# The last eight columns of T from on-chip tiles, and spread single-column products, in a Fourier-filter and feed-forward kernel

## The chip, the cores and the metric

The kernel runs on one core of a Trainium2 chip. The metric is the device time of one execution in microseconds. Before the change three runs took 1841.04, 1837.14 and 1839.90 us; their median is 1839.90.

## What is computed

The input x has 8192 tokens of 448 channels. A row c of 448 numbers makes six modulation rows. First comes a layer norm, scaled and shifted by two of them, then a Fourier filter over the tokens with a small complex network per frequency, and then a layer norm and a gated feed-forward network:

```python
mod = (_silu(c) @ w_mod).reshape(c.shape[0], 6, 1, -1)
sa, ca, ga, sb, cb, gb = (mod[:, 0], mod[:, 1], mod[:, 2], mod[:, 3], mod[:, 4], mod[:, 5])
h = _layernorm(x, axis=-1) * (1 + ca) + sa
x = x + ga * _A_ref(h, A_w1, A_b1, A_w2, A_b2)   # rfft2, two complex layers in 4 blocks of 112, soft threshold, irfft2
h = _layernorm(x, axis=-1) * (1 + cb) + sb
x = x + gb * _B_ref(h, B_w_gate, B_w_up, B_w_down)   # (gelu(h @ w_gate) * (h @ w_up)) @ w_down
```

## The kernel before, in words

The transform of 8192 = 128 x 64 tokens is made in two steps. The **first stage** takes x as 64 *columns* of 128 tokens each. Column b lies in chunk b // 4; a chunk is a tile xt of 128 partitions, four columns and 448 channels, and there are 16. For each column VectorE (or ScalarE for a few) makes the statistics of the layer norm; for a group of columns a chain on ScalarE (q, a square root) and VectorE gives the factor y (L421 to L427); an engine scales the 128-point matrix by y (fr, L190); TensorE multiplies the column by it (dft_a, L199, product at L201); and ScalarE copies the product back over the column, with a correction mu for the mean (out_a, L204; means, L208, product at L210). The result, called T, so stands in the tiles xt: 128 rows of frequencies by 64 columns.

T is also stored to DRAM (td), because the second stage needs it with the columns on the partitions. store_t (L366) writes a chunk: the first four chunks whole, of the others at first only quarter c = 0, the tile's partitions 0, 4, 8 and so on, which are T's rows 0 to 31 in td. The other quarters are written later, in the second stage.

The order of all of the first stage is made by a small planner. task (L377) notes an engine, a cost, a due time and what a step depends on; in_order (L387) plays the tasks through and gives one order, which is written out as it stands. Beside the columns the planner places:

- mod_terms on VectorE (L225) and mod_cols (L261, product at L266): eight products of one column each, which turn the modulation rows sa and ca into columns. bounds1, scale_sum (L299), scale_of and modulated make the scale of the first network layer and its scaled weights w1m; weights1_hi and weights1_lo split these into two float16 parts.
- dc_cols (L276, product at L281): eight more products of one column, for the term of frequency zero.
- the stores of all 16 chunks, issued on SyncE.

Behind the planner's tasks, in the order in which the code is written, stand the steps that open the **second stage** (L795 on). It works on 32 *units* (h, bt), a half of the channels and a block of eight rows of T. fetch_t (L504) loads a unit's tile tr from td: partitions 0 to 63 are the 64 columns for one row parity o, 64 to 127 those for the other, and along a partition lie four rows of 224 channels. There are three tr buffers; they come from a pool that is opened after the first stage's pool `ap` is closed and takes its place in memory. The first three units are fetched at L796. Then mod_row (L237, product at L247) makes the modulation rows sb and cb, four products each; row_copy and weights2_hi prepare the second network layer, and split_t (L519) splits units 0 and 1 into float16 parts th and tl on ScalarE and VectorE. From then on step (L733) takes one unit after another: it fetches unit i + 2, makes the 64-point transform of unit i (stage_s2), splits unit i + 1 on GpSimd, and runs the network and the inverse transform for the units before (stage_m1, stage_m2, stage_i1). On TensorE the order at the start is: transform of unit 0, of unit 1, first layer of unit 0, transform of unit 2, second layer of unit 0 (L626 to L633). weights2_lo and weights2_turn give that layer's low part w2l; its turn on GpSimd (L333, L334) stands behind the split of unit 2.

SyncE issues every transfer in one queue. There are eight semaphores for them, so a transfer waits until the one eight places ahead of it has landed.

Later stages, which the change doesn't touch, load and pack the feed-forward weights, finish the inverse transform and run the feed-forward network.

Of the kernel before, what the change touches and what calls it, by code (L numbers as in the profile page):

```python
# [12 lines left out]
F16 = mybir.dt.float16  # L13
# [37 lines left out]
def spectral_geglu(ctx, tc, x, wa, wb, wg, wu, wd, cvec, wmod, wmod3, cf1, cs2, cmi, cgm, out):  # L51
    nc = tc.nc
    V, S, G, T = nc.vector, nc.scalar, nc.gpsimd, nc.tensor
    dma = nc.sync.dma_start
# [5 lines left out]
    td = dram.tile([128, NB, D], F32, name="td")  # L60
# [9 lines left out]
    def bank(tag, name):  # L70
        return (psumc if tag == "pc" else psum).tile([128, 512], F32, tag=tag, name=name)
# [72 lines left out]
    with ExitStack() as actx:  # L144
        ap = actx.enter_context(tc.tile_pool(name="ap", bufs=1, side="right"))
        xts = {}
# [41 lines left out]
        frs, psb, psu = {}, {}, {}  # L188
# [48 lines left out]
        def mod_row(h, ks):  # L237

            if h not in rps:
                rps[h] = bank("pd", "psm")  # L240
            for k in ks:
                c = slice(2 * h, 2 * h + 2)
                if k < 3:
                    a, w = cs[:, k : k + 1].to_broadcast([128, 128]), wn[:, c, k]
                else:
                    a, w = cs[64:128, 3:4].to_broadcast([64, 128]), w3[64:128, c]
                T.matmul(rps[h][:, :D].rearrange("p (h c) -> p h c", h=2), a, w, start=k == 0, stop=k == 3)  # L247
# [5 lines left out]
        sa0 = lp.tile([112, NBLK], F32, name="sa0")  # L253
# [4 lines left out]
        wsc = cpool.tile([128, 2], F32, name="wsc")  # L258
        col2 = mpool.tile([113, 1], F32, name="col2")

        def mod_cols():  # L261

            ps = bank("pc", "psm")
            psu["m"] = ps
            for b in range(2 * NBLK):
                T.matmul(  # L266
                    ps[:112, b : b + 1], ms[:, b // 2, b % 2 * BS : (b % 2 + 1) * BS], ones[:, 0:1], start=True, stop=True
                )
# [4 lines left out]
            V.tensor_scalar(sa0, ps[:112, 0:4], float(N) * 2.0**-ZSC, None, op0=ALU.mult)  # L273
            V.tensor_scalar(ca1[:112], ps[:112, 4:8], 1.0, None, op0=ALU.add)

        def dc_cols():  # L276

            ps = psu["d"] = bank("pc", "psd")
            for r in range(2):
                for k in range(NBLK):  # L280
                    T.matmul(ps[:112, 4 * r + k : 4 * r + k + 1], wt[0][:112, r, k, :], sa0[:, k : k + 1], start=True, stop=True)  # L281

        def dc_out():
            V.tensor_scalar(hb, psu.pop("d")[:112, : 2 * NBLK], wsc[:112, 0:1], None, op0=ALU.mult)
# [70 lines left out]
        def load_mlp():  # L355
            for l, w in enumerate((wa, wb)):
                dma(wt[l][:112], w[:112])
                dma(wt[l][112:113], w[112:113])
            dma(mi, cmi)
# [52 lines left out]
        for r in (range(a, e) for a, e in zip([0] + ends, ends)):  # L412
# [7 lines left out]
            g, n = slice(r[0], r[-1] + 1), r[0]  # L420
            c = task("S", 0.3, (n, -2.0), [known[b][0] for b in r], S.activation, q[:, g], mv[:, g, 1], AF.Sqrt, eps)  # L421
            for fn, *args in (
# [5 lines left out]
                c = task("V", 0.1, (n, -1.8), [c], fn, *args)  # L428
            m = task(
                "G",  # L430
                0.2,
                (n, 0),
                [c] + [known[b][-1] for b in r],
                lambda g: G.tensor_tensor(nm[:, g], mv[:, g, 0], y[:, g], ALU.mult),
                g,
            )
            nms.update({b: m for b in r})
            mos = {}
            for cg in [cg for cg in cgroups if r[0] <= cg[-1] <= r[-1]]:
                n = cg[0] if cg[0] >= r[0] else cg[-1] + 1  # L440
# [7 lines left out]
            for b in r:  # L448
# [2 lines left out]
                done[b] = task("T", 1.5 if b < 2 else 0.75, (b, 0), [f] + [moved[i] for i in (b - 6,) if i >= 0], dft_a, b)  # L451
                if b in mos:
                    moved[b] = task("S", 0.53, (b + 6, -0.9), [mos[b], done[b]], out_a, b)
        for ch in range(NB // 4):
            task("P", 0.1, (4 * ch + 3, 0), [moved[b] for b in range(4 * ch, 4 * ch + 4)], store_t, ch, None if ch < CE else 0)

        ms_ = []
        for k in range(4):
            for h in range(2):
                ms_ = [task("V", 0.36 if k == 0 else 0.6, (57, k - 4), ms_, mod_terms, k, h, ready=49.0)]  # L460
        mx = [task("V", 1.0, (58, l - 3), [], mlp_max, l, ready=42.0) for l in range(2)]
        mc = task("T", 0.8, (61, 0), ms_, mod_cols)
        mco = task("V", 0.2, (61, 0.5), [mc], mod_cols_out)
        b1_ = task("V", 1.2, (61, 0.6), [mco] + mx, bounds1)
        s1 = task("T", 0.2, (63, 0.7), [b1_], scale_sum, 0)
        md = task("V", 1.0, (64, 0.5), [mco], modulated)
        s1o = task("V", 0.6, (63, 0.8), [s1], scale_of, 0, 4)
        dc = task("T", 0.8, (64, 0.5), [mco, s1], dc_cols)
        bd2 = task("V", 0.7, (64, 0.2), [s1o], bounds2)
        dco = task("V", 0.2, (64, 0.6), [dc, bd2], dc_out)  # L470
        wh = task("S", 1.05, (64, 1.0), [s1o, md], weights1_hi)
        wl = task("V", 1.15, (64, 3.0), [wh], weights1_lo)
        task("G", 2.2, (64, 2.0), [wh], weights1_neg, w1h)
# [5 lines left out]
        with tc.manual_schedule():  # L479
            silu_c()  # L480
            G.memset(ones, 1.0)
            load_x(0, 0, 1)
            load_x(0, 1, 1)
            dma(f1c, cf1)
            load_x(0, 2, 2)
            for ch in range(1, NB // 4):
                load_x(ch)
            load_mlp()
            load_mods()
            dma(s20, cs2[:, BTS[0] * GB : (BTS[0] + 1) * GB])  # L490
            V.memset(ca1, 1.0)
            V.memset(cm, 1.0)
            for fn, args in in_order():
                fn(*args)


    with ExitStack() as bctx:
# [6 lines left out]
        def fetch_t(h, bt):  # L504
            raw = bp1.tile([128, GB, HC], F32, tag="tr", name="tr", bufs=3)
            r = BTS.index(bt) * 2 * GB
            dma(raw, td[r : r + 2 * GB, :, h * HC : (h + 1) * HC].rearrange("(g o) b c -> (o b) g c", o=2))
# [9 lines left out]
            trs[(h, bt)] = raw, s2s.pop((h, bt))  # L517

        def split_t(h, bt, el=G):  # L519
# [206 lines left out]
        units = [(h, bt) for bt in bts[:-4] for h in range(2)] + [(h, bt) for h in range(2) for bt in bts[-4:]]  # L726
# [66 lines left out]
                store_us(*u)  # L793

        ctx.enter_context(tc.manual_schedule())  # L795
        for u in units[:3]:  # L796
            fetch_t(*u)
        zh = [bp1.tile([113, 2, ZW], F16, name=f"zh{i}") for i in range(4)]
        hh_ = [bp1.tile([113, 2, ZW], F16, name=f"hh{i}") for i in range(4)]
        for z in zh:  # L800
            S.activation(z[96:113, 0], ones[96:113], AF.Copy, scale=2.0**-ZSC)
        for z in hh_:
            G.tensor_copy(z[96:113, 0], ones[96:113])
        mod_row(0, range(4))
        mod_row(1, range(4))

        n = NB // 4
        late = [(ch, c) for ch in range(CE, n - 6) for c in range(1, NC)] + [(ch, 1) for ch in range(n - 6, n)]
# [378 lines left out]
    with ExitStack() as cctx:  # L1187
# [647 lines left out]
        def store_forms(t, part):  # L1835
# [226 lines left out]
        for u in range(U0, NT_ + 1):  # L2062
            period(u)
            i, k = divmod(u, NP)
# [119 lines left out]
```

## Time and profile before

| | us |
|---|---|
| median of 3 runs | 1839.90 |
| profiled execution | 1842.18 |
| its span | 1840.0 |
| TensorE busy | 1804.4 |
| VectorE busy | 1400.8 |
| GpSimd busy | 1326.2 |
| ScalarE busy | 997.6 |

Times in the trace are microseconds from the span's start. A row of the timeline gives the start, the duration, the engine, the line, the operation, the tiles written and read, and how many instructions were merged; in brackets stands how long the engine had been idle before it and what ended that. One float32 product on TensorE shows as two records. A row of the chain of waits gives start, duration and what was running. SPq is SyncE's queue: its rows are the time that the issue of a transfer took, not the transfer itself. "PEclk" is the granted TensorE clock, 1.00 at full speed.

### The profile page before, as it was taken

How to read it: one execution, taken by the hardware profiler on the slowest of the kernel's cores; microseconds unless marked ns; L12 is line 12 of the kernel's file. 1: busy time of each engine (PE TensorE's matmuls, PEld its weight loads, DVE VectorE, ACT ScalarE, POOL GpSimd, SP SyncE). 2: the span in 40 equal slices, each digit the busy share in tenths (PEclk: the TensorE clock that was granted, in tenths of full speed). 3: DMA queues.
4: the chain of work that ended last, by engine and by line, in shares of the span. 5: the costliest groups of instructions: out<-in, count | busy, mean ns of one | idle time of the engine just before them, and what ended most of it. 6: DMA issues, size and time to landing. Idle time of an engine off the chain costs nothing.

```text
span 1840.0 us, 56044 instructions
## 1 busy us (share of the span) xinstructions
PE 1804.4 (98%) x23042; PEld 1707.7 (93%) x23042; DVE 1400.8 (76%) x2924; ACT 997.6 (54%) x1934; POOL 1326.2 (72%) x1763
## 2 busy tenths in 40 slices
PE   7999999899999999999999999999999999999998
PEld 3699999688888889999999999999999999999998
DVE  8699999778766767777777777777777777777755
ACT  7677787544444444555555555555555555555543
POOL 4467888158777778777777777777777777777644
PEclk9999999899999999999999999999999999999999
DMA  9889778644444445966677666666666666666661
GB/s 361 309 285 305 235 210 229 198 102 105 106 106 105 105 105 140 287 174 174 174 174 174 174 175 178 180 182 178 175 176 180 181 181 178 180 179 178 154 170 56
DMA packets 382996, 332.02 MB, mean 180 GB/s; under 512 B 114354, under 2 KB 361010, under 8 KB 382484
## 3 DMA queue, kind: packets, MB, share of 16 engines
q1 hardware_dynamic: 382740, 328.45, 64.6%
q8 instruction: 180, 2.95, 0.7%
q14 instruction: 76, 0.62, 0.1%
HBM read 243.32 MB, written 60.10 MB: 165 GB/s over the span
## 4 chain that ended last, share of the span: by engine, by line
PE 87%; DVE 5%; DMA 3%; ACT 2%; POOL 2%; issue 1%; SPq 0%; ACTq 0%; DVEq 0%; POOLq 0%
PE set L1591 37%; PE pgu L1335 11%; PE pdn L1408 6%; PE pdn L1410 6%; PE pdn L1409 6%; PE ps L201 2%; PE set L1408 2%; PE set L1409 2%; PE set L1410 2%; DVE y L649 1%; DMA wk<-wk 1%; PE set L1715 1%; PE pm L601 1%; PE pm L603 1%; PE pm L608 1%
## 5 line engine op out<-in xcount | busy, mean ns | idle before, releaser
L1591 PE MATMUL set<-nt,wk 128*128 128x128 f16 x12768 | 719.9, 219 | 3.2 <-DMA wk<-wk 2.3
L1591 PEld LDWEIGHTS <-wk 128*128 128x128 f16 x12768 | 715.9, 98 | 5.0 <-DMA wk<-wk 2.7
L1410 PE MATMUL pdn<-wd,ac 128*128 128x224 f16 x1218 | 315.5, 259 | 0.6 <-DVE ac L1396 0.6
L1408 PE MATMUL pdn<-wd,ac 128*128 128x224 f16 x1218 | 315.7, 259 | 0.0
L1409 PE MATMUL pdn<-wd,ac 128*128 128x224 f16 x1218 | 315.5, 259 | 0.0
L1335 PE MATMUL pgu<-nt,wk 128*128 128x256 f16 (+1 forms) x2464 | 269.5, 274 | 3.4 <-DVE x L1376 3.3
L1335 PEld LDWEIGHTS <-wk 128*128 128x128 f16 (+1 forms) x2464 | 226.6, 98 | 44.7 <-issue 18.3
L1640 ACT ACTIVATE gl<-c,dg 128x384 f32<-128x384 f32 x168 | 103.1, 614 | 241.6 <-DVE c L1634 238.4
L1666 DVE SCALAR_TENSOR_TENSOR ac<-x,sa_act,ac 128x896 f16<-128x896 f32 x168 | 205.1, 1221 | 35.7 <-ACT ac L1656 35.7
L1384 POOL TENSOR_TENSOR x<-x 128x128 f32<-128x128 f32 x223 | 129.3, 580 | 109.5 <-DVE x L1376 60.8
L1656 ACT ACTIVATE ac<-x,sa_act 128x896 f16<-128x896 f32 x168 | 174.8, 1040 | 53.6 <-POOL x L1387 47.3
L1385 POOL TENSOR_TENSOR x<-x 128x128 f32<-128x128 f32 x223 | 186.0, 834 | 17.5
L1454 POOL TENSOR_TENSOR cq<-cq 128x224 f32<-128x224 f32 x32 | 21.0, 658 | 236.8 <-DVE cq L1453 236.8
L1386 POOL TENSOR_TENSOR x<-x 128x128 f32<-128x128 f32 x223 | 172.7, 775 | 0.0
L1644 DVE TENSOR_TENSOR x<-c,gl 128x384 f32<-128x384 f32 x168 | 143.8, 856 | 21.6 <-ACT gl L1640 20.6
L1408 PEld LDWEIGHTS <-ac 128*128 128x128 f16 x1568 | 153.4, 98 | 4.9 <-issue 4.8
L1410 PEld LDWEIGHTS <-ac 128*128 128x128 f16 x1568 | 153.4, 98 | 0.8 <-DVE ac L1396 0.8
L1409 PEld LDWEIGHTS <-ac 128*128 128x128 f16 x1568 | 153.5, 98 | 0.1
L1387 POOL TENSOR_TENSOR x<-x 128x128 f32<-128x128 f32 x223 | 142.7, 640 | 0.0
L1628 DVE TENSOR_TENSOR c<-set,sb 128x512 f32<-128x512 f32 x168 | 115.1, 685 | 26.4 <-PE set L1591 24.9
L1371 ACT ACTIVATE gel<-pgu,dg 128x256 f32<-128x256 f32 x112 | 49.7, 470 | 139.1 <-PE pgu L1335 131.4
L117 POOL TENSOR_TENSOR yl<-y,yh 128x448 fp32r<-128x448 f32 x63 | 90.0, 1444 | 46.2 <-ACT yh L115 44.1
(351 smaller groups left out, 3781.7 us busy)
## 6 DMA issues: line engine op xcount, KB each, us to landing
wk<-wk SPq DMA_DIRECT2D x76, 1024.0 KB, 9.3
wk<-wk SPq DMA_DIRECT2D x76, 768.0 KB, 6.5
tr<-td SPq DMA_DIRECT2D x32, 448.0 KB, 5.2
vd<-us SPq DMA_DIRECT2D x64, 224.0 KB, 3.1
xx<-in_A_x SPq DMA_DIRECT2D x32, 448.0 KB, 6.1
v<-vd SPq DMA_DIRECT2D x63, 224.0 KB, 5.7
out<-x SPq DMA_DIRECT2D x31, 448.0 KB, 3.3
xt<-in_A_x SPq DMA_DIRECT2D x15, 896.0 KB, 15.8
```

The lines of the kernel that those rows point to most:

```text
L1335: T.matmul(pgu[i, t, q][:, pr * H : (pr + 1) * H], ws[rows, n, w, tw], nts[i][rows, tn, :], start=start, stop=stop, skip_group_check=True,)
L1384: e.tensor_tensor(s1, a21, a22, ALU.add)
L1385: e.tensor_tensor(s2, s1, a11, ALU.subtract)
L1386: e.tensor_tensor(s3, a11, a21, ALU.subtract)
L1387: e.tensor_tensor(s4, a12, s2, ALU.subtract)
L1408: T.matmul(ps, ac[:, 0, ka], w[:, 0, kb], start=n == 0, stop=False)
L1409: T.matmul(ps, ac[:, 0, ka], w[:, 1, kb], start=False, stop=False)
L1410: T.matmul(ps, ac[:, 1, ka], w[:, 0, kb], start=False, stop=n == NP - 1)
L1591: T.matmul(ps2[:, pr, reg * 128 : reg * 128 + 128], slot[:, pr, hl, wt, :], nt[:, xt, :], start=start and j == 0, stop=j == len(terms) - 1 ...
L1644: V.tensor_tensor(xs[u][:, 1::3, :], cts.pop(u)[:, 1], gls.pop(u), ALU.mult)
L1656: S.activation(ac[:, 0], xs[u][:, 0:7], AF.Copy, scale=sa_act[:, t : t + 1])
L1666: V.scalar_tensor_tensor(ac[:, 1], xs.pop(u)[:, 0:7], sa_act[:, t : t + 1], ac[:, 0], op0=ALU.mult, op1=ALU.subtract)
```

## The change

There are three edits. The shown diff leaves out the new line numbers of what only moved.

1. Units 0 and 1 (fetch_t, for the first block): the tile is loaded from td for columns 0 to 55 only, in one transfer for each row parity. A new function last_columns fetches the columns 56 to 63 from the tiles of chunks 14 and 15, one transfer for each unit, parity and column: 16 for a chunk, each of one partition with four rows of 224 numbers (3.5 KB). The store of chunk 15's first quarter is taken out of the planner and stands behind them; the fetch of unit 2 comes after it.
2. mod_cols and dc_cols are cut into four tasks of two products each, with due times of their own, and mod_row's eight products become eight tasks of the planner.
3. Sixteen products of 128 x 512 on a tile of ones, whose result nobody reads, stand ahead of the first column.

```diff
-        def mod_cols():
+        def mod_cols(b0):
-            for b in range(2 * NBLK):
+            for b in range(b0, b0 + 2):
...
-        def dc_cols():
+        def dc_cols(n):
...
-        for ch in range(NB // 4):
+        for ch in range(NB // 4 - 1):
             task("P", 0.1, (4 * ch + 3, 0), [moved[b] for b in range(4 * ch, 4 * ch + 4)], store_t, ch, None if ch < CE else 0)
...
-        mc = task("T", 0.8, (61, 0), ms_, mod_cols)
+        mc = [task("T", 0.3, (59 + n, 0.3), ms_, mod_cols, 2 * n) for n in range(NBLK)]
...
-        dc = task("T", 0.8, (64, 0.5), [mco, s1], dc_cols)
+        for n in range(2 * NBLK):
+            task("T", 0.75, (64, 0.3 + 0.8 * n), [], mod_row, n // 4, (n % 4,), ready=52.0)
+        dc = [task("T", 0.3, (64, 0.5 + 0.8 * n), [mco, s1], dc_cols, 2 * n) for n in range(NBLK)]
...
             G.memset(ones, 1.0)
+            ps = bank("pa", "pwarm")
+            o16 = ones.bitcast(F16)
+            for _ in range(16):
+                T.matmul(ps, o16[:, 0:128], o16[:, 0:512], start=True, stop=True)
...
             r = BTS.index(bt) * 2 * GB
-            dma(raw, td[r : r + 2 * GB, :, h * HC : (h + 1) * HC].rearrange("(g o) b c -> (o b) g c", o=2))
+            hc = slice(h * HC, (h + 1) * HC)
+            if bt == BTS[0]:
+                n = NB - 8
+                for o in range(2):
+                    dma(raw[o * 64 : o * 64 + n], td[r + o : r + 2 * GB : 2, :n, hc].rearrange("g b c -> b g c"))
+                firsts.append((raw, hc))
+            else:
+                dma(raw, td[r : r + 2 * GB, :, hc].rearrange("(g o) b c -> (o b) g c", o=2))
...
+        def last_columns(ch):
+            for raw, hc in firsts:
+                for o in range(2):
+                    for b in range(4):
+                        p = o * 64 + 4 * ch + b
+                        dma(raw[p : p + 1], xts[ch][4 * o : 32 : 8, b, hc])
...
-        for u in units[:3]:
+        for u in units[:2]:
             fetch_t(*u)
+        for ch in (NB // 4 - 2, NB // 4 - 1):
+            last_columns(ch)
+        store_t(NB // 4 - 1, 0)
+        fetch_t(*units[2])
...
-        mod_row(0, range(4))
-        mod_row(1, range(4))
```

More of the change, by code (lines that the diff above doesn't have):

```diff
@@ L259, in spectral_geglu @@
         col2 = mpool.tile([113, 1], F32, name="col2")
-        def mod_cols():
-            ps = bank("pc", "psm")
-            psu["m"] = ps
-            for b in range(2 * NBLK):
+        def mod_cols(b0):
+            if b0 == 0:
+                psu["m"] = bank("pc", "psm")
+            ps = psu["m"]
+            for b in range(b0, b0 + 2):
                 T.matmul(
@@ L274, in mod_cols_out @@
             V.tensor_scalar(ca1[:112], ps[:112, 4:8], 1.0, None, op0=ALU.add)
-        def dc_cols():
[L278 to L281, printed above, removed]
+        def dc_cols(n):
+            if n == 0:
+                psu["d"] = bank("pc", "psd")
+            ps = psu["d"]
+            for b in range(n, n + 2):
+                r, k = divmod(b, NBLK)
+                T.matmul(ps[:112, b : b + 1], wt[0][:112, r, k, :], sa0[:, k : k + 1], start=True, stop=True)
         def dc_out():
@@ L461, in spectral_geglu @@
         mx = [task("V", 1.0, (58, l - 3), [], mlp_max, l, ready=42.0) for l in range(2)]
-        mc = task("T", 0.8, (61, 0), ms_, mod_cols)
-        mco = task("V", 0.2, (61, 0.5), [mc], mod_cols_out)
+        mc = [task("T", 0.3, (59 + n, 0.3), ms_, mod_cols, 2 * n) for n in range(NBLK)]
+        mco = task("V", 0.2, (61, 0.5), mc, mod_cols_out)
         b1_ = task("V", 1.2, (61, 0.6), [mco] + mx, bounds1)
@@ L467, in spectral_geglu @@
         s1o = task("V", 0.6, (63, 0.8), [s1], scale_of, 0, 4)
-        dc = task("T", 0.8, (64, 0.5), [mco, s1], dc_cols)
+        for n in range(2 * NBLK):
+            task("T", 0.75, (64, 0.3 + 0.8 * n), [], mod_row, n // 4, (n % 4,), ready=52.0)
+        dc = [task("T", 0.3, (64, 0.5 + 0.8 * n), [mco, s1], dc_cols, 2 * n) for n in range(NBLK)]
         bd2 = task("V", 0.7, (64, 0.2), [s1o], bounds2)
-        dco = task("V", 0.2, (64, 0.6), [dc, bd2], dc_out)
+        dco = task("V", 0.2, (64, 0.6), dc + [bd2], dc_out)
         wh = task("S", 1.05, (64, 1.0), [s1o, md], weights1_hi)
@@ L517, in fetch_t @@
             trs[(h, bt)] = raw, s2s.pop((h, bt))
+        firsts = []
+        def last_columns(ch):
[4 more added lines that the diff above has]
+                        dma(raw[p : p + 1], xts[ch][4 * o : 32 : 8, b, hc])
         def split_t(h, bt, el=G):
```

## The prediction

> **What bounds the kernel now.** First the page: the span, the engines' busy time, and the chain that ended last.
>
> ```profile
> span 1840.0 us, 56044 instructions
> PE 1804.4 (98%) x23042; PEld 1707.7 (93%) x23042; DVE 1400.8 (76%) x2924; ACT 997.6 (54%) x1934; POOL 1326.2 (72%) x1763
> PE 87%; DVE 5%; DMA 3%; ACT 2%; POOL 2%; issue 1%; SPq 0%; ACTq 0%; DVEq 0%; POOLq 0%
> ```
>
> TensorE is the bound, with 35.6 us of the span not busy. The change touches the first 90 us alone, and what it does to the moment at which TensorE gets past them is what the end will move by. The table by stretches (columns PE, PEld, DVE, ACT, POOL busy, granted clock, DMA share) shows the stages there:
>
> ```profile
> 16.00:24.00 8.00, 6.34 (x19) 3.06 (x20) 7.61 (x32) 7.25 (x19) 3.64 (x9) 1.00 1.01 421
> 24.00:60.00 36.00, 35.69 (x116) 18.85 (x115) 35.75 (x126) 29.66 (x59) 19.73 (x39) 1.00 1.02 393
> 66.00:72.00 6.00, 5.89 (x14) 2.98 (x14) 3.00 (x11) 3.04 (x7) 2.97 (x3) 0.72 0.17 69
> 90.00:100.00 10.00, 10.00 (x110) 9.99 (x109) 8.65 (x16) 6.23 (x11) 6.84 (x6) 1.00 0.92 315
> ```
>
> Until 24 us VectorE and ScalarE are the full engines; then TensorE is full until 60, and again from 90 on. Between lies the hand-over from the columns to the units. There I read the chain of waits in order of time:
>
> ```profile
> 71.16 0.64 ACT xt L206
> 71.82 2.88 DMA td<-xt
> 74.98 0.40 SPq L507
> 75.43 0.50 SPq L507
> 75.98 7.12 DMA tr<-td
> 83.26 2.26 POOL th L115
> 85.59 1.88 POOL tl L117
> 87.47 1.29 POOL w2l L333
> 88.77 0.52 POOL w2l L334
> 89.33 0.26 PE pm L629
> ```
>
> The last copy of a column ends at 71.8, its store lands at 74.7, three fetches of T go out, and the third (unit 2's) lands at 83.26. GpSimd splits it, then turns w2l, and TensorE, which waits for w2l, runs on at 89.33. So unit 2's data sets the pace, not unit 0's or 1's: these were there from 78.66 and 79.98.
>
> ```profile
> 78.66 0.94 ACT L115 CAST th<-tr 128x896 f16<-128x896 f32 x1 [2.46 <-DMA tr<-td]
> 79.98 0.94 ACT L115 CAST th<-tr 128x896 f16<-128x896 f32 x1 [0.38 <-DMA tr<-td]
> ```
>
> The yardstick is therefore the 89.33. The profiled execution took 1842.18 us for its span of 1840.0; the median of the runs is 1839.9. I put the shift of the 89.33 on the median.
>
> **The 16 idle products.** TensorE's rows in order of time:
>
> ```profile
> 8.50 5.21 PE L201 MATMUL ps<-xt,fr 128*128 128x448 f32 x8 [8.50 <-DVE fr L196]
> 22.89 0.99 PE L201 MATMUL ps<-xt,fr 128*128 128x448 f32 x2 [0.25 <-ACT xt L206]
> 23.86 3.25 PE L201 MATMUL ps<-xt,fr 128*128 128x448 f32 x8
> 58.43 1.64 PE L266 MATMUL psm<-ones,ms 128*112 128x1 f32 x16
> 64.02 1.71 PE L281 MATMUL psd<-sa,wt 112*112 112x1 f32 x16
> 66.16 4.97 PE L201 MATMUL ps<-xt,fr 128*128 128x448 f32 x8
> 76.93 1.01 PE L247 MATMUL psm<-w,cs 64*128 64x448 f32 x2
> ```
>
> Four columns (two records each) take 5.21 us at 8.50 and 3.25 at 23.86: the start loses 1.96. The idle products need only a memset at 0.9 us, so they are over before 8.5 even if all run slowly, and cost nothing. What they give is at most 1.96 and I take 0: at 22.89 TensorE waits for a copy on ScalarE, which is 7.25 of 8 us busy there, and in the order written out its copies stand behind statistics that wait for x, whoever is early. The Trainium skill's page "TensorE: Matmul & The Clock Gate" (Part 1: The HAM clock gate) has the array at half rate until some 3.4 us of activity; by that the 1.96 are won at TensorE, and the 5.21 agree.
>
> **Single-column products and the second slow stretch.** Two more rows by stretches:
>
> ```profile
> 67.50:70.00 2.50, 2.50 (x5) 1.06 (x4) 0.88 (x2) 1.03 (x2) 1.81 (x2) 0.50 0.04 14
> 81.00:84.00 3.00, 3.00 (x30) 3.00 (x31) 2.81 (x4) 1.45 (x3) 0.74 (x1) 0.50 1.00 383
> ```
>
> Behind the eight products of L281 the clock is halved and the last four columns take 4.97 instead of 3.25. Spread out, I expect this gone: 1.7 us. The order on TensorE, before, from mod_cols' products (psm) to the last column, with dc_cols' (psd), some columns left out:
>
> ```order
> L266 MATMUL psm<-ones,ms 112x1 x8
> L201 MATMUL ps_761<-xt_142,fr 128x448
> L210 MATMUL psmu<-nm,f_156 128x4
> L201 MATMUL ps_785<-xt_142,fr 128x448
> L281 MATMUL psd<-sa_167,wt_149 112x1 x8
> L201 MATMUL ps_826<-xt_143,fr 128x448
> L201 MATMUL ps_843<-xt_143,fr 128x448
> ```
>
> and now (L247 is a row product):
>
> ```order
> L267 MATMUL psm<-ones,ms 112x1 x2
> L201 MATMUL ps_774<-xt_142,fr 128x448
> L201 MATMUL ps_793<-xt_142,fr 128x448
> L267 MATMUL psm<-ones,ms 112x1 x6
> L247 MATMUL psm<-wn,cs 128x448
> L201 MATMUL ps_822<-xt_143,fr 128x448
> L201 MATMUL ps_841<-xt_143,fr 128x448
> L284 MATMUL psd<-sa_167,wt_149 112x1 x4
> ```
>
> The dc products now stand behind the last column. On VectorE the factors y of the last group moved ahead of the chain of bounds, which made them late:
>
> ```profile
> 58.77 0.14 DVE L426 SCALAR_TENSOR_TENSOR y<-t,q 128x4 f32<-128x4 f32 x1
> 65.17 0.15 DVE L426 SCALAR_TENSOR_TENSOR y<-t,q 128x4 f32<-128x4 f32 x1
> ```
>
> So the last copy, step by step: chunk 14's columns start at 59.2 (its y at 58.77 and a scaled matrix), four columns 3.1, six products 6/8 of 1.64 = 1.2, one row product like a column 0.8, four columns and a means product 3.2, the copy 0.6: 59.2 + 8.9 = 68.1 instead of 71.8. This gains 3.7. The seven row products that are left run behind it, under the transfers; a gap of TensorE follows, since its work then ends near 76.
>
> **The fetches.** SyncE's queue before, from the stores of the last two chunks to the first of the later stores:
>
> ```order
> L372 DMA td<-xt_142 32x1792 [waits DMAHW3_49,Activation_49]
> L372 DMA td<-xt_143 32x1792 [waits DMAHW4_49,Activation_49]
> L507 DMA tr<-td 128x4x224 [waits DMAHW3_49,DMAHW4_49,DMAHW2_49,DMAHW5_49,DMAHW1_49,DMAHW6_49,DMAHW0_49,DMAHW7_49,PE_49,Pool_49]
> L507 DMA tr<-td 128x4x224 x2
> L512 DMA s_867<-cs 128x1024
> L372 DMA td<-xt_132 32x1792 x3
> ```
>
> and now (tr are the units' tiles, xt_142 and xt_143 the chunks 14 and 15; of 32 pieces four are shown):
>
> ```order
> L375 DMA td<-xt_142 32x1792 [waits DMAHW3_49,Activation_49]
> L520 DMA tr<-td 56x4x224 [waits DMAHW4_49,DMAHW2_49,DMAHW5_49,DMAHW1_49,DMAHW6_49,DMAHW0_49,DMAHW7_49,Activation_49,Pool_49]
> L520 DMA tr<-td 56x4x224 x3
> L543 DMA tr<-xt_142 1x4x224 x3
> L543 DMA tr<-xt_143 1x4x224 [waits DMAHW0_49]
> L375 DMA td<-xt_143 32x1792 [waits DMAHW0_49]
> L523 DMA tr<-td 128x4x224 [waits DMAHW1_49,DMAHW0_49]
> ```
>
> Two things stand here. The first fetch waits for ScalarE still, though not for the store of chunk 15; that chunk's pieces wait for no ScalarE of their own, so the wait ahead of them must be that for the last copy. The tiles tr lie where the first stage's pool lay, and its last reader is that copy. So nothing of the early fetch happens before 68.1. And unit 2's fetch, the one that counts, stands behind 4 + 32 transfers and the store of chunk 15, whose landing it awaits. Rows for the price of one issue on SyncE (min/median/max in ns), and for the landing of the transfers out of tile us, to which L1140 belongs:
>
> ```profile
> 74.98 1.50 SPq L507 DMA_DIRECT2D tr<-td  x3
> L358 SPq DMA_DIRECT2D wt<-in_A_wb x2: 229/252/276, 28.0 to 32.4; - x2
> L1140 SPq DMA_DIRECT2D v<-us x8: 492/548/647, 328.1 to 342.0; - x8
> DMA to landing us min/median/max: 2.9/3.1/4.9
> ```
>
> Large ones cost 0.50 back to back. A piece is one row of 3.5 KB on chip. L358 is one row too, but alone on the queue: 0.25. L1140 goes from tile to tile, back to back: 0.55, with a gap 0.60. No row shows a piece; I take s = 0.40, between them, nearer to neither. Eight are in flight, so landings of 3.1 would bound s by 0.39 as well.
>
> The Trainium skill's page "DMA: Bandwidth & Descriptors" (Issuing engines are not separate DMA queues) calls the sequencer's time to start a transfer usually small beside the transfer. The three fetches agree (0.50 against 3.7 to landing); for pieces this small I go by the rows. By the rule s would be at its lower end, 0.25, and the time 1840.6.
>
> Now the sum. Last copy 68.1; four fetches of 0.5: 70.1; 32 pieces: 82.9; the store to the next fetch as before (71.82 to 74.98) 3.16: 86.1; unit 2's landing: unit 0's took 3.7 at an idle queue (74.98 to 78.66), unit 2's 7.3 behind two others (75.98 to 83.26); nothing is ahead now, so 4.0: 90.1. GpSimd's split took 2.25 for th beside VectorE's w2l, and 0.94 undisturbed:
>
> ```profile
> 83.44 1.27 DVE L344 SCALAR_TENSOR_TENSOR w2l<-wt,col,w2h 113x448 f16<-113x448 f32 x2
> 83.26 2.25 POOL L115 CAST th<-tr 128x896 f16<-128x896 f32 x1 [5.07 <-DMA tr<-td]
> 89.47 0.94 POOL L115 CAST th<-tr 128x896 f16<-128x896 f32 x1 [0.19 <-DMA tr<-td]
> ```
>
> Now w2l is over when unit 2 lands, so the 6.07 from 83.26 to 89.33 become 4.76: 94.8. That is 5.5 later than 89.33. In a formula: shift = 32 s - 7.3. The units 0 and 1 get their last piece at about 80 and 83 plus a landing, also later than 78.66 and 79.98, but TensorE is through with them before unit 2 is split.
>
> The later queue of stores and weight loads moves by about as much; it had 0.9 MB of fetches ahead of it that are now out of the way, so I add nothing for it. From 90 on TensorE is full, so the shift stays to the end.
>
> **The rivals.** About 3.7 us (0.2%) is what a measurement of this kernel tells from no change.
>
> 1. The queue of pieces is what counts (forecast): s 0.345 to 0.5, shift 3.7 to 8.7, 1845.4 at 0.40. For it: every back-to-back row costs 0.5. Chance 0.56.
> 2. Pieces are cheap: s from 0.25 to 0.345; the 3.7 us gained at the columns pay for them. Shift 0.7 to 3.7, 1842 us, no change. For it: L358. Against: that row never stood behind another. Chance 0.27.
> 3. Faster: the head start of 1.96 gets through to the last copy, and pieces cost less than any row shows, s below 0.18: 32 x 0.18 - 7.3 - 1.96 = -3.5, so 1836 or less. It decides at s = 0.17. Against: ScalarE's 7.25 of 8, and 229 ns as the least issue. Chance 0.07.
> 4. Dear pieces, s 0.5 to 0.6 as L1140: shift 8.7 to 11.9, 1850. Chance 0.10. Unit 2's landing of 7.3 instead of 4.0 would come to this too.
> 5. Within 1: TensorE pauses from 76 to about 83, and the clock is halved behind it as in 81:84; units 0 and 1 then take up to 1.7 us more, and if unit 2's split doesn't cover it the time is 1847. The pause ahead of that row was 1.7 us; the skill's clock page (same section) has it behind an idle window of some 3.4. I give it a tenth of case 1.
>
> **The numbers.** Likeliest: 1839.9 + 5.5 = 1845.4. The range goes from s just under 0.25 with two fifths of the head start (1839.9 + 0.7 - 0.8 and 0.5 of scatter: 1839.3) to s = 0.58 (+11.3: 1851.2). Slower 0.56 + 0.10 = 0.66, same 0.27, faster 0.07.
>
> **What would show it.** Right: a last copy near 68; no 0.50 clock at 67 to 70; the first tr fetch right behind that copy; 32 rows of L543 of about 0.4 each; unit 2's split on GpSimd at about 90 and the first L655 that waits for w2l near 94.8. Wrong: pieces through by 79; TensorE resuming before 90; or a fetch issued before the last copy.

## The result, and the profile after

The changed kernel takes 1853.52 us (median of four runs, 1848.01 to 1854.23), the kernel before 1839.28 (four runs, 1837.14 to 1841.04). The ratio is 1.0071, with a 95% interval of 1.0049 to 1.0094: 14 us slower. The forecast was 1845.4, with a range to 1851.2. The direction holds and so does the path that was forecast, the queue of pieces; the size does not. The profiled execution took 1854.23.

From the page of the kernel after, the span and the shares of the chain that ended last:

```profile
span 1852.2 us, 56117 instructions
PE 86%; DVE 4%; DMA 3%; ACT 2%; POOL 2%; SPq 2%; issue 1%; ACTq 0%; DVEq 0%; POOLq 0%
```

SyncE's queue (SPq) had 0% of that chain before and has 2% now: the time went into issuing transfers. ScalarE's last copies of columns, and then SyncE's queue in order of time from there on:

```profile
64.56 2.79 ACT L206 ACTIVATE xt<-ps,mu 128x448 f32<-128x448 f32 x4
```

```profile
70.04 1.74 SPq L520 DMA_DIRECT2D tr<-td  x4
71.82 20.35 SPq L543 DMA_DIRECT2D tr<-xt  x32
92.22 0.51 SPq L375 DMA_DIRECT2D td<-xt  x1
94.44 0.42 SPq L523 DMA_DIRECT2D tr<-td  x1
```

The last copy ends at 67.35. The four fetches go out at 70.04, then the 32 pieces hold the queue for 20.4 us, to 92.22: 0.64 for each. Behind them stand chunk 15's store and, at 94.44, unit 2's fetch. The view of a single line gives the price of one issue (min/median/max in ns):

```profile
L543 SPq DMA_DIRECT2D tr<-xt x32: 572/573/734, 71.8 to 91.6; - x32
L520 SPq DMA_DIRECT2D tr<-td x4: 363/413/418, 70.0 to 71.4; - x4
```

A piece of 3.5 KB costs more to issue than a fetch of 56 rows (573 ns against 413). The view of what SyncE waits for between 55 and 100 us has no row of L543: the pieces don't wait for one another to land. The rest of the path, from GpSimd's row and some rows of the chain of waits in order of time:

```profile
98.29 0.93 POOL L115 CAST th<-tr 128x896 f16<-128x896 f32 x1 [22.55 <-DMA tr<-td]
```

```profile
91.60 1.68 DMA tr<-xt
93.38 0.95 ACT th L115
94.37 0.35 PE ps L565
99.31 1.89 POOL tl L117
101.20 1.30 POOL w2l L336
103.06 0.26 PE pm L655
```

Unit 2 lands at 98.29, 3.85 behind its issue; GpSimd had been idle for 22.55 us. TensorE gets w2l at 103.06, against 89.33 before: 13.7 us later, close to the 14.2 us between the medians. Part of that closeness is chance: of the same two profiled executions the spans differ by 12.2 us, and the first product of the last stage (L1591 before, L1619 after) starts 11.4 us later, at 747.2 instead of 735.8. The chain leads back to the last piece and not to unit 2's fetch: its landing at 93.28 lets unit 1's th begin. Two paths of nearly the same length end here, and both go through the 32 pieces.

The table by stretches of the kernel after (PE, PEld, DVE, ACT, POOL busy, granted clock, DMA share, GB/s):

```profile
66.00:72.00 6.00, 6.00 (x31) 3.87 (x30) 2.43 (x9) 4.15 (x8) 3.47 (x2) 1.00 0.44 164
76.00:80.00 4.00, 0.00 (x0) 0.00 (x0) 0.00 (x0) 0.00 (x0) 0.00 (x0) 0.77 0.03 7
80.00:84.00 4.00, 0.00 (x0) 0.00 (x0) 0.00 (x0) 0.00 (x0) 0.00 (x0) 0.50 0.02 5
96.00:100.00 4.00, 4.00 (x32) 4.00 (x32) 3.54 (x11) 1.69 (x3) 1.62 (x2) 0.67 1.00 378
```

The first row shows the good half of the change: the clock is 1.00 where it was 0.72. The second and third show all the engines idle while the DMA engines are 2 to 3% busy: not the transfers are slow, their issue is. Meanwhile the granted clock falls to 0.50, and it is back at 1.00 only within the last row.

### The profile page after: what moved, and what is told of

It is laid out like the page before. It is cut to its first block, busy times and chain, and to the rows that moved or that the text cites. A ratio compares the mean times of both kernels' runs of the same rounds, so it can differ in the third digit from the quotient of the medians.

```text
span 1852.2 us, 56117 instructions
## 1 busy us (share of the span) xinstructions
PE 1806.6 (98%) x23058; PEld 1709.4 (92%) x23058; DVE 1397.0 (75%) x2924; ACT 999.0 (54%) x1934; POOL 1325.6 (72%) x1763
## 4 chain that ended last, share of the span: by engine, by line
PE 86%; DVE 4%; DMA 3%; ACT 2%; POOL 2%; SPq 2%; issue 1%; ACTq 0%; DVEq 0%; POOLq 0%
PE set L1619 37%; PE pgu L1363 11%; PE pdn L1436 6%; PE pdn L1438 6%; PE pdn L1437 6%; PE ps L201 2%; PE set L1436 2%; PE set L1437 2%; PE set L1438 2%; DVE y L675 1%; SPq L543 1%; PE pm L627 1%; PE pm L629 1%; PE ps L565 1%; PE pm L628 1%
## 5 line engine op out<-in xcount | busy, mean ns | idle before, releaser
L1619 PE MATMUL set<-nt,wk 128*128 128x128 f16 x12768 | 719.7, 219 | 3.9 <-DMA wk<-wk 3.1
L1619 PEld LDWEIGHTS <-wk 128*128 128x128 f16 x12768 | 715.9, 98 | 5.7 <-DMA wk<-wk 3.4
L675 DVE SCALAR_TENSOR_TENSOR y<-pm,lam,t 64x224 f32<-64x224 f32 x256 | 114.9, 449 | 8.8 <-ACT t L667 4.8
```

Source lines behind the costliest of these rows:

```text
L675: V.scalar_tensor_tensor(y[ri * 64 : ri * 64 + 64, gi], pv[si, ri], lam[si, 0:1], tv[si, ri], op0=ALU.add, op1=ALU.min)
L1619: T.matmul(ps2[:, pr, reg * 128 : reg * 128 + 128], slot[:, pr, hl, wt, :], nt[:, xt, :], start=start and j == 0, stop=j == len(terms) - 1 ...
```

## Experiments

"The moment of w2l" is the start of the TensorE product that takes what GpSimd's turn of w2l leaves, one profiled execution each: the yardstick of the prediction. In e4 and e12 that product doesn't wait for the turn, which is over by then. The times of the kernel before are those measured beside the kernel of the row, on the same chip. The shift of the moment and that of the time agree to 3 us in all rows but e5, where they differ by 4.2.

| kernel | moment of w2l | median us (runs) | before | ratio, 95% interval |
|---|---|---|---|---|
| before | 89.33 | 1839.28 (4) | | |
| after | 103.06 | 1853.52 (4) | 1839.28 | 1.0071 [1.0049, 1.0094] |
| e1: edits 2 and 3, no pieces | 83.29 | 1835.86 (10) | 1839.04 | 0.9982 [0.9972, 0.9992] |
| e2: edit 1 alone | 106.65 | 1853.77 (4) | 1839.04 | 1.0084 [1.007, 1.0097] |
| e5: edit 3 alone | 87.60 | 1840.57 (12) | 1838.06 | 1.0012 [1.0003, 1.0021] |
| e6: edit 2 alone | 82.75 | 1833.84 (12) | 1838.06 | 0.9975 [0.9965, 0.9984] |
| e11: after without edit 3 | 101.26 | 1850.17 (6) | 1840.46 | 1.0054 [1.004, 1.0068] |
| e3: pieces on two queues | 100.88 | 1850.82 (4) | 1839.04 | 1.0069 [1.005, 1.0089] |
| e4: unit 2 fetched first | 102.84 | 1852.37 (4) | 1839.04 | 1.0077 [1.0063, 1.0091] |
| e9: 16 pieces | 93.15 | 1843.16 (10) | 1840.46 | 1.0019 [1.0009, 1.0028] |
| e10: 8 transfers of four rows | 89.08 | 1840.62 (10) | 1840.46 | 1.0 [0.9989, 1.001] |
| e12: e6 and an early w2l | 84.05 | 1834.20 (6) | 1840.70 | 0.9963 [0.9949, 0.9977] |

### The three edits by themselves

**e1**: fetch_t and the planner's stores as before, edits 2 and 3 kept.

```diff
-        for u in units[:2]:
+        for u in units[:3]:
             fetch_t(*u)
-        for ch in (NB // 4 - 2, NB // 4 - 1):
-            last_columns(ch)
-        store_t(NB // 4 - 1, 0)
-        fetch_t(*units[2])
...
```

> Units 0 and 1 are fetched whole from DRAM again, the other two edits stay. Theory Q (the queue: unit 2's fetch stands behind 32 pieces on SyncE, each 0.62 us): the last copy stays at 67.4 us, its store and the first fetch follow as in the kernel before (3.2 us later, 70.5), unit 2 lands near 78 and TensorE gets its w2l near 84 instead of 89.3: about 5 us faster than before, 1834. Rival S (the gain at the columns is lost elsewhere, so the hand-over is not what these edits move): 1839, as before.

It took 1835.86. Without the pieces what is left of the change is faster than before, so the pieces cost some 17 us within the changed kernel.

**e2**: edit 1 alone; the products stand as in the kernel before. Against the kernel after, in part:

```diff
-        mc = [task("T", 0.3, (59 + n, 0.3), ms_, mod_cols, 2 * n) for n in range(NBLK)]
+        mc = task("T", 0.8, (61, 0), ms_, mod_cols)
...
-            for _ in range(16):
-                T.matmul(ps, o16[:, 0:128], o16[:, 0:512], start=True, stop=True)
...
```

> The kernel before with the pieces alone. Theory Q: the last copy as before at 71.8, no store to wait for, the first fetch at 72; from there to w2l 33 us as in the changed kernel (70.0 to 103.1): w2l at 105, 15.6 us slower than before, 1855. Rival (a piece costs the 0.40 of the prediction, and the rest of the 14 us comes from the spread products): 9 us slower, 1848.

It took 1853.77. SyncE's queue shows the same 20.4 us, only later, since the columns end later:

```profile
72.29 3.12 SPq L511 DMA_DIRECT2D tr<-td  x4
75.45 20.37 SPq L534 DMA_DIRECT2D tr<-xt  x32
```

What stays odd: the moment of w2l is 106.65, 3.6 later than in the kernel after, and the time is the same. The traces show where the difference goes. The first product of the feed-forward network (pgu) still starts 3.8 us later, at 367.6 instead of 363.8; the first product of the last stage (set) starts only 0.2 later, at 747.4 instead of 747.2. Between them the granted clock over 400 to 410 us is 0.83 in the kernel after and 1.00 in e2, which is worth up to 1.7 us. The rest is open.

**e5**: the 16 idle products alone.

```diff
             G.memset(ones, 1.0)
+            ps = bank("pa", "pwarm")
+            o16 = ones.bitcast(F16)
+            for _ in range(16):
+                T.matmul(ps, o16[:, 0:128], o16[:, 0:512], start=True, stop=True)
```

> The kernel before with the 16 idle products alone. Theory of the prediction (the engines of the statistics set the pace until 23 us): the first four columns take 3.3 instead of 5.2 us and the row at 22.9 stays within 0.3, no change, 1839.3. Rival (the head start gets through): 1.9 us earlier at 23 and at the end, 1837.4.

**e11**: the kernel after without these lines.

> The kernel after without the 16 idle products alone. Theory N (they are worth nothing in the end): 1853.5, within 1 us. Rival C (they cost 1.5 to 2.5 us, as the single runs with and without them so far hint: 1840.6 against 1838.1 and 1835.9 against 1833.8): 1851.5.

They gain nothing: e5 is 2.5 us over the kernel before, and e11, with 1850.17, is nearer to the rival's 1851.5 than to 1853.5. TensorE's first columns in e5:

```profile
9.52 3.46 PE L201 MATMUL ps<-xt,fr 128*128 128x448 f32 x8 [1.85 <-DVE fr L196]
```

The first four columns take 3.46 instead of 5.21, near the 3.25 of later ones, but they start no earlier: at 9.52, when VectorE has their scaled matrix. (Nor do they always run at that pace: in e3, which has the idle products too, the clock reads 0.66 over 8 to 12 us and the four columns take 4.97.) The row that stands at 22.89 in the kernel before stands at 23.56 in e5. From the first column to that row it is 14.04 us in e5, and 14.06 in e2 (9.27 to 23.33), which has no idle products. So the head start is used up by then, as the prediction had it.

That the products even cost something is hinted at three times (e5 over before; e1 over e6 by 2.0 us, or by 1.0 when each is taken against the kernel before measured beside it; after over e11 by 3.3), and only e5's interval excludes no difference. The traces don't show such a cost near the products. The profiled execution of e5 is shorter than that of the kernel before, with spans of 1838.8 and 1840.0. Those of e1 and e6 are level when the last stage begins (its first product at 726.1 and 726.0) and 3.1 apart at its last product (1816.1 and 1813.0). What the products cost stays open.

The trace of e5 shows one thing more. Its eight products of one column for frequency zero stand in one block, as in the kernel before, and yet the four columns behind them are not slow:

```profile
64.70 1.71 PE L281 MATMUL psd<-sa,wt 112*112 112x1 f32 x16
66.83 3.27 PE L201 MATMUL ps<-xt,fr 128*128 128x448 f32 x8
```

The granted clock over 67.5 to 70 us is 1.00 here, and 0.50 in the kernel before and in e2, with the same block. So this block was followed by the halved clock in two executions of three. Without it e5's four columns are done 1.0 us earlier than in the kernel before although they begin 0.7 later, and e5's moment of w2l, 87.60, is earlier than 89.33.

**e6**: the spread products alone.

```diff
+        mc = [task("T", 0.3, (59 + n, 0.3), ms_, mod_cols, 2 * n) for n in range(NBLK)]
+        for n in range(2 * NBLK):
+            task("T", 0.75, (64, 0.3 + 0.8 * n), [], mod_row, n // 4, (n % 4,), ready=52.0)
+        dc = [task("T", 0.3, (64, 0.5 + 0.8 * n), [mco, s1], dc_cols, 2 * n) for n in range(NBLK)]
...
```

> The kernel before with the spread products alone. Theory of the prediction: this edit alone makes the last copy come at 67.4 instead of 71.8, and the fetch 4 to 5 us earlier: 1834 to 1835, the same as with the idle products beside it. Rival (part of the gain at the last copy was the head start's): 1836.

It took 1833.84, 4.2 us under the kernel before, and beats both kernels. TensorE's rows around the last column, and SyncE's fetches, in e6:

```profile
62.92 0.92 PE L201 MATMUL ps<-xt,fr 128*128 128x448 f32 x2
63.81 2.50 PE L201 MATMUL ps<-xt,fr 128*128 128x448 f32 x6
67.12 0.86 PE L284 MATMUL psd<-sa,wt 112*112 112x1 f32 x8
```

```profile
69.45 1.50 SPq L519 DMA_DIRECT2D tr<-td  x3
```

The last four columns take 0.92 + 2.50 where they took 4.97 at the halved clock, the dc products come behind them, and the fetches go out at 69.45 instead of 74.98. The clock is only a part of this: against e5, where the block stays whole and the clock stays at 1.00, e6 still has w2l 4.85 us earlier. Of that 0.9 is a start of the columns that happened to be earlier. The rest comes with the order: the factors y of the last group are made at 61.88 in e6 and at 65.85 in e5, and the dc products no longer stand ahead of the last columns.

### What a piece pays for

**e7**: each piece reads from one partition instead of four.

```diff
-                        dma(raw[p : p + 1], xts[ch][4 * o : 32 : 8, b, hc])
+                        dma(raw[p : p + 1], xts[ch][p : p + 1, :, hc])
```

> The changed kernel, but each piece reads its 3.5 KB from one partition of the tile instead of from four, so units 0 and 1 get other numbers in their last eight columns. Theory F (the source over four partitions makes a piece dear): the issue falls from 0.57 to about 0.25 us, the 32 take 9 us and the time is 1843. Rival R (a piece of one destination row costs 0.57 wherever it reads): 0.57 and 1853.

**e8**: each piece reads the same numbers from T in DRAM.

```diff
-                        dma(raw[p : p + 1], xts[ch][4 * o : 32 : 8, b, hc])
+                        dma(raw[p : p + 1], td[o : 2 * GB : 2, 4 * ch + b, hc].rearrange("(u g) c -> u g c", u=1))
...
+            if ch == NB // 4 - 1:
+                store_t(ch, 0)
             last_columns(ch)
-        store_t(NB // 4 - 1, 0)
```

> The changed kernel, but each piece reads the same numbers from T in DRAM, with the store of chunk 15 ahead of that chunk's pieces. Theory N (a transfer from tile to tile is dear): the issue falls to 0.25 to 0.3 us as for the one-row load of the first stage, 1844. Rival R (one destination row costs 0.57 whatever it reads): 0.57 and 1852.

One run each: 1849.75 and 1854.19. The line of the pieces in e7, then in e8:

```profile
L543 SPq DMA_DIRECT2D tr<-xt x32: 567/567/737, 69.5 to 89.1; - x32
```

```profile
L543 SPq DMA_DIRECT2D tr<-td x32: 551/552/707, 70.7 to 92.0; - x32
```

567 and 552 ns instead of 573: neither the number of source partitions nor the on-chip source makes the price.

**e3**: every second piece is issued on ScalarE's queue.

```diff
-                        dma(raw[p : p + 1], xts[ch][4 * o : 32 : 8, b, hc])
+                        (dma if b % 2 else S.dma_start)(raw[p : p + 1], xts[ch][4 * o : 32 : 8, b, hc])
```

> The changed kernel with every second piece issued from ScalarE's queue. Theory Q: SyncE issues 16 pieces instead of 32, unit 2's fetch goes out 16 x 0.62 = 9.9 us earlier, 1843.6. Rival L (pieces are limited by their landing: eight in flight, 4.9 us each): both queues wait for the same eight semaphores, 1853.5 as the changed kernel.

It took 1850.82, with neither theory's number. The pieces on the two queues, and SyncE's queue in order of time:

```profile
L543 ACTq DMA_DIRECT2D tr<-xt x16: 580/582/1173, 68.0 to 82.8; - x16
L543 SPq DMA_DIRECT2D tr<-xt x16: 572/573/737, 78.5 to 89.4; - x16
```

```profile
75.49 1.97 SPq L520 DMA_DIRECT2D tr<-td  x4
78.45 11.54 SPq L543 DMA_DIRECT2D tr<-xt  x16
92.28 0.41 SPq L523 DMA_DIRECT2D tr<-td  x1
```

The price is the same on ScalarE, 582 ns. SyncE's half of the pieces takes about half the time, 11.5 us. But SyncE's fetches now start at 75.49 instead of 70.04, so its half begins only when most of ScalarE's is out, and the two queues do not run side by side for long. What SyncE waited for ahead of them is in its view of waits (total us, times, longest):

```profile
SPq L375 <- DMA tr<-xt: 5.8, 2, 5.2
```

A store ahead of the fetches waited up to 5.2 us for a piece that ScalarE had issued. ScalarE paid too: from 68.8 to 83.58 us it did none of its other work. The split of units 0 and 1 began at 88.85 and 91.19, against 88.43 and 93.38 in the kernel after.

**e9**: 16 pieces; columns 56 to 59 come from DRAM with the rest.

```diff
-                n = NB - 8
+                n = NB - 4
...
-        for ch in (NB // 4 - 2, NB // 4 - 1):
+        for ch in (NB // 4 - 1,):
```

> The kernel after with 16 pieces instead of 32: units 0 and 1 come from DRAM for columns 0 to 59, and only chunk 15's four columns come from the tile on chip. Theory Q (the price is so much per piece in SyncE's queue): 16 x 0.618 = 9.9 us less in the queue, so unit 2's fetch is issued near 84.6 instead of 94.4, and the time is 1853.5 - 9.9 = 1843.6. Rival P (the price is a pause of TensorE, after which its clock is halved, rather than the queue itself; a pause of 10 us halves it as one of 15 does): the time falls by clearly less than the queue, to 1847 or more, with a granted clock of 0.50 for the same stretch behind the pause.

**e10**: 8 transfers of four rows each.

```diff
-                    for b in range(4):
-                        p = o * 64 + 4 * ch + b
-                        dma(raw[p : p + 1], xts[ch][4 * o : 32 : 8, b, hc])
+                    p = o * 64 + 4 * ch
+                    dma(raw[p : p + 4], xts[ch][4 * o : 32 : 8, :, hc])
```

> The kernel after with the 32 pieces joined to 8 transfers of four partitions each. Such a transfer can't exchange partitions and columns, so it puts other numbers of the same tiles into the last eight columns of units 0 and 1: the output is not the reference's, the bytes moved are the same. Theory T (so much per transfer): 8 x 0.6 = 4.8 us in the queue instead of 20.35, unit 2's fetch near 79, TensorE gets w2l near 87.5, and the time is 1853.5 - 15.5 = 1838, level with the kernel before. Rival B (so much per row that is written): one transfer takes 2.3 us, the queue is as long as now, and the time is 1853.

They took 1843.16 and 1840.62. SyncE's queue in e9:

```profile
71.93 10.47 SPq L543 DMA_DIRECT2D tr<-xt  x16
84.68 0.42 SPq L523 DMA_DIRECT2D tr<-td  x1
```

and in e10, with the price of one:

```profile
71.95 5.67 SPq L542 DMA_DIRECT2D tr<-xt  x8
79.99 0.42 SPq L523 DMA_DIRECT2D tr<-td  x1
```

```profile
L542 SPq DMA_DIRECT2D tr<-xt x8: 637/638/835, 72.0 to 77.0; - x8
```

In e9 unit 2's fetch is at 84.68 where 84.6 was expected, and the time is 1843.16 where 1843.6 was (beside a kernel before that measured 1.2 higher there): the price is linear in the number of pieces. The rival's 1847 or more did not come, but its condition did not come either: the clock, at 0.50 for 20 us in the kernel after, is at 0.67 over 80 to 84 and 0.75 over 84 to 88 here. So e9 leaves open how much a longer pause would add. In e10 a transfer of four times the rows and bytes takes 638 ns, 65 more than a piece: the price is per transfer. With 5.67 us of issue in place of 20.35 the time is level with the kernel before. It missed 1838 by 2.6 us, and GpSimd's row and a stretch of e10 show a part of it (1.2 us is that the kernel before measured that much higher beside it):

```profile
83.91 1.34 POOL L115 CAST th<-tr 128x896 f16<-128x896 f32 x1 [8.27 <-PE ps L570]
```

```profile
80.00:84.00 4.00, 4.00 (x40) 4.00 (x39) 3.12 (x6) 1.82 (x5) 0.09 (x1) 0.50 0.73 234
```

Unit 2's split waited for TensorE's transform of an earlier unit, whose buffer it takes over, and TensorE ran at the halved clock behind its pause. The split began at 83.91 and took 0.4 us longer for th than in the kernel after. Unit 2's fetch itself was at 79.99, 1 us later than expected.

### Which unit counts, and what is next

**e4**: unit 2's fetch goes between the pieces of chunk 14 and those of chunk 15.

```diff
-        for ch in (NB // 4 - 2, NB // 4 - 1):
-            last_columns(ch)
         store_t(NB // 4 - 1, 0)
+        last_columns(NB // 4 - 2)
         fetch_t(*units[2])
+        last_columns(NB // 4 - 1)
```

> The changed kernel with the store of chunk 15 ahead of the pieces and unit 2's fetch between chunk 14's pieces and chunk 15's. Theory Q in its narrow form (only unit 2's fetch counts): it goes out at 82 instead of 94.4, w2l is turned near 91 and the time is 1841. Rival U (units 0 and 1 set the pace as soon as unit 2 does not): their last piece still lands at 93, TensorE needs 7 us from there to the second layer, 101 instead of 103, 1851.5.

It took 1852.37, 1.1 us under the kernel after. Its fetch of unit 2, ScalarE's th of unit 1, VectorE's w2l, the end of GpSimd's turn, and a stretch of TensorE:

```profile
81.15 0.45 SPq L523 DMA_DIRECT2D tr<-td  x1
82.19 9.85 SPq L543 DMA_DIRECT2D tr<-xt  x16
```

```profile
93.28 0.94 ACT L115 CAST th<-tr 128x896 f16<-128x896 f32 x1 [4.00 <-DMA tr<-xt]
```

```profile
96.46 1.27 DVE L347 SCALAR_TENSOR_TENSOR w2l<-wt,col,w2h 113x448 f16<-113x448 f32 x2
```

```profile
99.10 0.56 POOL L337 COPY w2l<-w2l 112x448 f16<-112x448 f16 x1
```

```profile
96.00:100.00 4.00, 4.00 (x26) 4.00 (x25) 3.42 (x9) 1.35 (x3) 1.84 (x2) 0.50 0.93 281
```

Unit 2 was fetched 13.3 us earlier, and the moment of w2l is 102.84 instead of 103.06. The last 16 pieces end at 92.04, as in the kernel after; unit 1's th waits for them, and VectorE's w2l stands behind that. GpSimd has turned w2l by 99.66, 3.4 us earlier than in the kernel after, but TensorE can't use it: from 94.27 on it is full with the units that came late, at half clock until 100. So unit 2's place in the queue is not the cause by itself: the pieces hold back units 0 and 1 by as much, and the halved clock adds to it.

**e12**: e6, with w2l made and turned ahead of the splits.

```diff
         weights2_hi()
+        weights2_lo()
+        weights2_turn(wv[1])
         for u in units[:2]:
             split_t(*u, el=V)
...
-        at(0, "act", weights2_lo)
-        at(1, "pool", weights2_turn, wv[1])
```

> The spread products alone (1833.8, 4.2 us under the kernel before in the same call), and on top the low part w2l is made on VectorE and turned on GpSimd ahead of the splits of units 0 to 2 instead of behind. In the trace of the spread products alone the w2l turn stands behind unit 2's split (th at 77.02, tl at 78.03 for 2.86 beside VectorE's w2l, turn 80.87 to 82.70), and TensorE runs on at 82.75. Theory Y (the moment at which TensorE gets w2l and runs on is the yardstick of the whole time): w2l is ready near 77.7, unit 2's split lasts until about 80.8 and is what TensorE waits for; TensorE resumes 2 us earlier, and the time is 2 us less, 1832 beside a kernel before of 1838. Rival O (something else of that stage, such as ScalarE's and VectorE's work for units 0 and 1, is level with w2l): the gap of TensorE at 82.75 is only moved, and the time stays at 1834.

It took 1834.20 beside 1840.70 for the kernel before, on another chip than e6; the ratio of 0.9963 is not to be told from e6's 0.9975. The gap only moved, as the rival had it. GpSimd's split and turn in e6:

```profile
78.03 2.86 POOL L117 TENSOR_TENSOR tl<-tr,th 128x896 f16<-128x896 f32 x1
80.87 1.32 POOL L336 TENSOR_SCALAR w2l<-w2l 112x448 f16<-112x448 f16 x1
```

and in e12, with TensorE's wait:

```profile
77.69 2.17 POOL L336 TENSOR_SCALAR w2l<-w2l 112x448 f16<-112x448 f16 x1
81.32 1.89 POOL L117 TENSOR_TENSOR tl<-tr,th 128x896 f16<-128x896 f32 x1
83.27 0.65 PE L567 MATMUL ps<-s,tl 128*112 128x128 f16 x8 [0.36 <-POOL tl L117]
```

The turn beside VectorE's splits took 2.17 where it took 1.32 in e6, unit 2's tl is over at 83.2 instead of 80.9, and TensorE waits for that instead. (The last column of this execution came 1.3 us later than e6's.)

## Why the prediction was wrong in size

Step by step, the forecast against the profiled execution of the kernel after:

| step | forecast | measured | later by |
|---|---|---|---|
| last copy of a column | 68.1 | 67.35 | -0.75 |
| first fetch | 68.1 | 70.04 | +1.9 |
| four fetches, to | 70.1 | 71.82 | +1.7 |
| 32 pieces, to | 82.9 | 92.22 | +9.3 |
| store, to unit 2's fetch | 86.1 | 94.44 | +8.3 |
| unit 2 lands | 90.1 | 98.29 | +8.2 |
| TensorE gets w2l | 94.8 | 103.06 | +8.3 |

**The step that failed** is "No row shows a piece; I take s = 0.40, between them, nearer to neither." The term 32 x s was 12.8 us and measured 20.4: s is 0.64, of which 0.573 is the issue. That is 7.6 of the 8.3 us. With 0.636 in its place the prediction's own formula gives 32 x 0.636 - 7.3 = 13.1 and 1853.0. Of the two bounds L358 was the wrong one. It is one row of 3.5 KB too, but in one run of bytes and alone on the queue; a piece is read in four runs and stands in a row of pieces. e7 and e8 rule out the number of source partitions and the place of the source; which of the differences that are left makes the price no run shows. L1140 (0.548 for the issue, 0.60 with its gap) was nearest in kind, from tile to tile and back to back in pairs, and it would have given 32 x 0.6 = 19.2 and 1851.8. It stood there as rival 4, with a chance of 0.10, and the top of the range was drawn at 0.58, below the row. A rule of the Trainium skill had been weighed at this place: the page "DMA: Bandwidth & Descriptors" (Issuing engines are not separate DMA queues) calls the time to initiate a transfer usually small beside the transfer. The runs here do not bear that out: of the 1.68 us from the start of the last piece's issue to its landing 0.57 are issue, a third, and in 32 in a row the issues add up to 20.4 while the landings overlap.

**The first fetch** was rightly put behind the last copy, and not early, but it went 2.7 us behind that copy's end in this execution, not at once. In other executions of the same order (e4, e11) it is at 68.30 and 68.33. SyncE's queue in e11:

```profile
68.33 1.74 SPq L516 DMA_DIRECT2D tr<-td  x4
70.12 20.35 SPq L539 DMA_DIRECT2D tr<-xt  x32
```

In the kernel after, the view of waits of that line names the landing of a store of T (total us, times, longest):

```profile
SPq L520 <- DMA td<-xt: 2.0, 1, 2.0
```

The forecast had left those stores out.

**The store of chunk 15** took 2.22 to the next issue, not 3.16, and took back 0.9. **The landing** (3.85 for 4.0) and **the split with w2l** (4.77 for 4.76) were right.

**The spread products** came out as forecast: no stretch at 0.50 around 66 to 72 in any kernel that has them, a last copy 4.4 earlier than before for 3.7 forecast, and 4.2 us of time where they stand alone (e6). The reason is shown less well: the 1.7 us were put down to the block of single-column products, and e5 has the block without the halved clock.

**The idle products** at zero: right as a gain; whether they cost 1 to 3 us is open.

**Units 0 and 1** ("TensorE is through with them before unit 2 is split"): this is wrong as a reason that they don't count. In e4 they, and the halved clock that they meet, keep the moment of w2l at 102.84.

**From 90 on** ("so the shift stays to the end"): only in the main. The shift of 13.7 us at w2l is 11.4 at the last stage's first product and 12.2 at the end of the profiled execution.

**The clock after the pause** (rival 5) came, and larger. TensorE's last row ahead of its pause in the kernel after:

```profile
73.45 1.01 PE L247 MATMUL psm<-w,cs 64*128 64x448 f32 x2
```

Its work ends at 74.5; by the stretches the clock is at 0.50 from about 78 (0.77 over 76 to 80) to about 98.6 (0.67 over 96 to 100). The page "TensorE: Matmul & The Clock Gate" of the Trainium skill (Part 1: The HAM clock gate) lets the clock fall behind an idle window of some 3.4 us; the trace agrees, with about 3.7 from the last product to the fall. In the kernel after GpSimd waits for unit 2's landing and not for TensorE, so this is not what its split waits for; in e4 and e10 it is part of what ends last.

## What to carry to other kernels

Count the transfers that a change puts into a queue ahead of one that something waits for, and price each at the dearest row of the same kind, back to back, whatever its bytes: here 32 transfers of 3.5 KB held unit 2's fetch by 20 us to spare one store's way through memory. Before splitting a load to start it earlier, look whether the start is held by something else; here the tiles took the place of the first stage's, so it could not start before the last copy at all. And time the parts of a change apart: one of the three here was worth 4 us and was hidden under one that cost 17.

## What the runs showed of the hardware

- Issuing costs by the transfer and hardly by its size: 573 ns for one row from four partitions, 567 from one partition, 552 from DRAM, 638 for four rows, and 582 on ScalarE's queue; a fetch of 56 rows took 413 in the same stretch. Why a small one is dearer than a large one is not settled by these runs.
- GpSimd's turn of w2l took 2.17 us beside VectorE's splits (e12) and 1.32 in e6.
- A block of sixteen records of single-column products (1.6 to 1.7 us) stands twice in the kernel before, in e2 and in e5. The granted clock behind it was 0.50 in two of these six places (L281 in before and in the same block of e2) and 1.00 in four. In the eleven traces with smaller blocks it was 1.00 throughout 64 to 72 us.
- Behind 3.7 us without a product the granted clock fell to 0.50 in the kernel after, and in e4 TensorE still worked at that clock until 100 us.
